# One full-precision product in place of three split ones at the head of a projection kernel

## The chip, the cores and the metric

The kernel runs on one core of a Trainium2 chip. The metric is the device time of one execution, in microseconds (us). A core has a matrix engine (TensorE; PE in the profile, with its weight loads as PEld), a vector engine (VectorE, DVE), an activation engine (ScalarE, ACT), a general engine (GpSimd, POOL) and a queue that issues transfers (SyncE, SP). Each engine works through its own list of instructions in order and waits on semaphores where an operand comes from another engine or from a transfer.

## The reference

The input x has 2048 rows of 448 numbers. Two branches are mixed by a gate per row. One is linear attention with 16 heads of 28; the other is a long convolution (a state-space layer). Cut to what matters here:

```python
q, k, v = split_heads(x @ wqkv)
pq, pk = phi(q), phi(k)              # phi(t) = where(t > 0, t + 1, exp(t)) + 1e-6
kv = einsum("bhsd,bhse->bhde", pk, v)
z  = einsum("bhsd->bhd", pk)
o  = einsum("bhqd,bhde->bhqe", pq, kv) / (einsum("bhqd,bhd->bhq", pq, z)[..., None] + 1e-6)
a  = merge_heads(o) @ wo
b  = causal_conv(x, K) + x * D_skip
g  = sigmoid((x * gate_w).sum(-1, keepdims=True))
out = g * a + (1 - g) * b
```

The part that the change touches is the k part of `x @ wqkv`, for the first 128 rows of x.

## The kernel before, in words

The 2048 rows are worked in 16 chunks of 128 (`NC`). A projection of one chunk multiplies x, turned so that its 448 columns lie on partitions, with a weight matrix of 448 rows. The 448 are cut into four tiles (`J`): tiles 1, 2 and 3 hold 128 rows each, tile 0 the last 64, held twice.

Every operand exists in two halves. The high half is the number cast to fp32r, a shorter form of which TensorE takes a product of 448 columns in 0.20 us here, where one in fp32 stands at 0.95 us in the chain; the low half is what the cast lost (`low`: number minus high half). One product in fp32 precision is then a sum of three in fp32r: high x times high w (`hh`), low x times high w (`lh`), high x times low w (`hl`). Tile 0 has both halves of w in one tile, so it needs no `hl` of its own. This makes 4 + 4 + 3 = 11 products for a projection, each with 448 columns, summed in one PSUM tile (`pieces`; `project` runs all 11).

The names that matter at the head of the program:

- `turned[c]` is the landed fp32 copy of chunk c, turned; `wkr[j]` the landed fp32 tile j of the k weights. They come in three transfers (`PARTS`): chunk 0 with tile 1, then tiles 2 and 3, then tile 0 with chunk 1.
- `xt[c]` holds the two halves of a turned chunk, `wkh` and `wkl` those of the k weights (in the trace, tiles xt and wk; landed data lie in tile y).
- `split_w(j)` casts weight tile j on ACT and calls `low_w(j)`, which takes the low half on the engine named, here DVE. `split_t(c)` casts a turned chunk on ACT and takes its low half on POOL; `split_n(c)` does the same for the chunk as it is (tile xn).
- `fill(n)` issues n dummy products of 512 columns of a bf16 tile of ones (`warm`) into an unused PSUM tile. `WARM` of them stand first on TensorE.
- `k_feature`, `k_high` and `k_low` make phi(k) of a chunk and its two halves (tiles pkh, pkl); `do_g` multiplies x with them.

The order on each engine is that of the code: the schedule is written out by hand. At the head it is: dummies; on ACT the cast of tile 1; on DVE the halves of chunk 0 and the low half of tile 1; then tiles 2, 3 and 0; the projection of chunk 0; those of chunks 1 and 2; then the features of chunk 0, and so on. The projection of chunk 0 runs in the order that `last == "w"` gives: tile 1, tile 2, the low half of tile 1, tile 3, the low halves of tiles 2 and 3, and tile 0 last. Dummies stand behind its first, second and ninth product.

Of the kernel before, what the change touches and what calls it, by code (L numbers as in the profile page):

```python
# [15 lines left out]
P = 128  # L16
S = 2048
D = 448
# [7 lines left out]
LO = NAT + D  # L26
XC = LO + 64
NX = XC - NAT + D
WARM = 9
PARTS = ((("x", 0), ("w", 1)), (("w", 2), ("w", 3)), (("w", 0), ("x", 1)))  # L30
FIRST = 2 * NAT + J * D
QA = 1
# [98 lines left out]
def gated_mix_kernel(ctx: ExitStack, tc: tile.TileContext, xin, wq_d, wv_d, wo_d, abc_d, ldt_d, dsk_d,  # L131
                     tri_d, ident_d, mask_d, gcat_d, sel_d, first_d, gin_d, lag_d, out):
    nc = tc.nc
    PE, ACT, DVE, POOL, SP = nc.tensor, nc.scalar, nc.vector, nc.gpsimd, nc.sync
# [15 lines left out]
    wkh, wkl = wk2[:, 0], wk2[:, 1]  # L150
# [31 lines left out]
    xt, xn, turned, plain = {}, {}, {}, {}  # L182
# [10 lines left out]
    wkr = {}  # L193
# [29 lines left out]
    def low(eng, o, r, h):  # L223
        eng.tensor_tensor(out=o, in0=r, in1=h.bitcast(F32), op=ALU.subtract)  # L224

    def split_t(c):
        w = xt[c] = xt_p.tile([P, 2 * NAT], F32R, name="xt", tag="t")
        ACT.copy(w[:, :NAT], turned[c])  # L228
        low(POOL, w[:, NAT:], turned[c], w[:, :NAT])

    def split_n(c):
        r, w = plain[c], xn_p.tile([P, NX], F32R, name="xn", tag="n")
        xn[c] = w
        ACT.copy(w[:, :XC - NAT], r)  # L234
        low(POOL, w[:, XC - NAT:], r[:, :D], w[:, :D])
        if c > 2:
            skip(c)

    def skip(c):
        POOL.tensor_tensor(out=y[:, c], in0=plain[c][:, :D], in1=dsk, op=ALU.mult)  # L240
# [3 lines left out]
    def fill(n):  # L244
        for _ in range(n):
            PE.matmul(idle, lhsT=warm[:, :P], rhs=warm, start=True, stop=True)  # L246

    fill(WARM)
    ACT.activation(oks, warm[:DJ, :1], AF.Exp)

    def split_w(j, h, l, w, eng):
        ACT.copy(h[:, j], w[j] if isinstance(w, dict) else w[:, j])
        low_w(j, h, l, w, eng)

    def low_w(j, h, l, w, eng):
        r = slice(0 if j else 64, P)
        w = w[j] if isinstance(w, dict) else w[:, j]
        low(eng, (l if j else h)[r, j], w[r], h[r, j])
# [44 lines left out]
    def pieces(c, wh, wl, n, tag, last=None):  # L303
        o = ps.tile([P, 512], F32, name=tag, tag=tag)
        h, l = ([xt[c][:, i + k * P:i + (k + 1) * P] for k in range(J)] for i in (0, NAT))
        hh, lh, hl = ([(a[k], w[:, k]) for k in range(J)] for a, w in ((h, wh), (l, wh), (h, wl)))
        hl = hl[1:]
        if last == "x":
            seq = hh + hl + lh
        else:  # L310
            seq = [p for k in range(J) for p in (hh[k], lh[k])] + hl
            if last == "w":
                seq = seq[2:6] + seq[8:9] + seq[6:8] + seq[9:] + seq[:2]

        def run(count):
            for _ in range(min(count, len(seq))):
                a, b = seq.pop(0)
                run.n += 1
                PE.matmul(o[:, :n], lhsT=a, rhs=b, start=run.n == 1, stop=not seq)  # L319
        run.n = 0  # L320
        return o, run

    def project(*args, **kw):
        o, run = pieces(*args, **kw)
        run(11)
        return o
# [15 lines left out]
    def k_feature(c, o):  # L342
        e = tp.tile([P, D], F32, name="e", tag="e")
        pks[c] = o[:, :D]
        ACT.activation(e, pks[c], AF.Relu, scale=-1.0)  # L345
        ACT.activation(e, e, AF.Exp, scale=-1.0)  # L346
        DVE.scalar_tensor_tensor(out=pks[c], in0=pks[c], scalar=1.0, in1=e, op0=ALU.add, op1=ALU.max)  # L347

    def k_high(c):
        pkh[c] = tp.tile([P, D], F32R, name="pkh", tag="pkh")  # L350
        ACT.add(pkh[c], pks[c], 1e-6)

    def k_low(c):
        pk = pks.pop(c)
        pkl[c] = tp.tile([P, D], F32R, name="pkl", tag="pkl")
        for o, a, op in ((pkl[c], pkh[c].bitcast(F32), ALU.subtract), (zb, zb, ALU.add))[::-1 if c == NC - 1 else 1]:
            DVE.scalar_tensor_tensor(out=o, in0=pk, scalar=1e-6, in1=a, op0=ALU.add, op1=op)
# [56 lines left out]
    w = xt[0] = xt_p.tile([P, 2 * NAT], F32R, name="xt", tag="t")  # L414
# [1 line left out]
    ACT.copy(wkh[:, 1], wkr[1])  # L416
    DVE.tensor_copy(w[:, :P], turned[0][:, :P])
    low(DVE, w[:, NAT:], turned[0], w[:, :NAT])
    low_w(1, wkh, wkl, wkr, DVE)
    for j in (2, 3, 0):  # L420
        split_w(j, wkh, wkl, wkr, DVE)
    ko, run = pieces(0, wkh, wkl, D, "k", "w")
    for n, f in ((1, 1), (1, 1), (6, 0), (1, 1), (2, 0)):
        run(n)
        fill(f)
    ko = [ko]
    split_t(1)
    ko.append(project(1, wkh, wkl, D, "v0", "x"))
    split_t(2)
    ko.append(project(2, wkh, wkl, D, "v1", "x"))  # L430
    k_feature(0, ko[0])
    k_high(0)
    split_n(0)
    k_low(0)
    k_feature(1, ko[1])
    split_n(1)
# [21 lines left out]
    for c in range(2, NC - 2):  # L458
# [9 lines left out]
        ko = project(c + 1, wkh, wkl, D, "v1" if c in (2, 4) else "k")  # L468
# [33 lines left out]
        for j in {11: (0, 1), 12: (2, 3)}.get(c, ()):  # L502
            w = xn_p.tile([P, NX], F32R, name="wo", tag="n")[:DJ, :2 * D].rearrange("p (i d) -> p i d", i=2)
# [57 lines left out]
    def gates_b(g, tag):  # L561
        n = g.shape[1]
        o = ps.tile([P, 512], F32, name="o2", tag="v1")
        PE.transpose(o[:n, :P], g, ident)
        w = tp.tile([P, D], F32R, name="phs", tag=tag)[:n, :3 * P].rearrange("p (i t) -> p i t", i=3)
        phs.append(w)
        ACT.copy(w[:, 0:2], o[:n, None, :P].to_broadcast([n, 2, P]))
        return lambda: DVE.tensor_tensor(out=w[:, 2], in0=o[:n, :P], in1=w[:, 0].bitcast(F32), op=ALU.subtract)
# [46 lines left out]
    c = NC - 2  # L615
    gate(0, c)
    ko = project(c + 1, wkh, wkl, D, "k")
# [18 lines left out]
    last = gates_b(g2, "pkl")  # L636
# [7 lines left out]
    for i in range(4):  # L644
        do_g(c + 1, (i,))
        ACT.copy(gs[i], g[i][:, :D])
    qo, q_run = pieces(c + 1, wqh, wql, D + 2, "q")
    for i in range(5):
        phi(i)
# [234 lines left out]
```

## Time and profile before

| what | value |
|---|---|
| time, median of 3 runs | 179.49 us (179.27 to 180.06) |
| the profiled execution's own time | 179.93 us |
| its span in the trace | 178.1 us |
| TensorE busy | 172.5 us, 97% of the span |
| POOL / DVE / ACT busy | 67% / 65% / 53% of the span |
| first dummy product starts | 1.47 us |
| first real product's weight load | 5.39 us |
| projection of chunk 1 begins | 8.99 us |

The time of an execution is that of the device. The span goes from the first to the last instruction that the trace shows; 179.93 - 178.1 = 1.8 us lie around it. All times of rows are counted from the span's start.

### The profile page before, as it was taken

To read this page: it belongs to the slowest core of one execution; us is meant where nothing else is said; L and a number is where in the kernel's file an instruction comes from. 1 tells how busy PE (TensorE), PEld (TensorE's weight loads), DVE (VectorE), ACT (ScalarE), POOL (GpSimd) and SP (SyncE) were. 2 spreads that over 40 slices of the span, in tenths; PEclk is the share of its full clock that TensorE was granted. 3 is DMA by queue.
4 is the path that set the end of the run, shared out by engine and by line. 5 is a ranking of instruction groups with operands and counts; after the bars stand their busy time and mean duration, and the time that the engine had idled before them with its cause. 6 is when DMAs were issued, how large, how long until landed. Compare 5 with 4: busy or idle time off the path is not lost.

```text
span 178.1 us, 2750 instructions
## 1 busy us (share of the span) xinstructions
PE 172.5 (97%) x879; PEld 152.0 (85%) x879; DVE 115.9 (65%) x238; ACT 94.7 (53%) x212; POOL 119.5 (67%) x124
## 2 busy tenths in 40 slices
PE   6999999999999999999999999999999999999991
PEld 2598999999999999999989999877879999899990
DVE  1747647688857173562824519389799999998551
ACT  3779388884537244372536653444565455564441
POOL 3167577879259969687598999059289998773100
PEclk9999999999999999999999999999999999999999
DMA  5999974198003303033033000000031221131222
GB/s 166 416 291 271 249 203 153 10 375 239 4 1 118 118 0 120 5 118 101 18 118 122 0 0 0 0 4 5 6 60 68 88 98 62 67 119 73 109 76 82
DMA packets 7784, 18.40 MB, mean 103 GB/s; under 512 B 1755, under 2 KB 4520, under 8 KB 7768
## 3 DMA queue, kind: packets, MB, share of 16 engines
q1 hardware_dynamic: 7720, 18.16, 32.2%
q8 instruction: 7, 0.11, 0.3%
q10 hardware_dynamic: 48, 0.06, 0.2%
q14 instruction: 9, 0.07, 0.1%
HBM read 14.20 MB, written 3.67 MB: 100 GB/s over the span
## 4 chain that ended last, share of the span: by engine, by line
PE 91%; DVE 5%; issue 1%; ACT 1%; ACTq 0%
PE g L388 20%; PE q L319 19%; PE a L602 16%; PE k L319 15%; PE v L319 6%; PE tr L577 3%; PE q L246 3%; PE v L396 2%; PE v L395 2%; PE m L671 1%; DVE th L585 1%; DVE ot L607 1%; DVE den L527 1%; DVE den L522 1%; PE tr L691 1%
## 5 line engine op out<-in xcount | busy, mean ns | idle before, releaser
L602 PE MATMUL a<-wk,th 128*128 128x448 f32 (+1 forms) x170 | 39.5, 364 | 0.0
L388 PE MATMUL g<-pkh,xn 128*128 128x448 f32 x112 | 36.1, 370 | 0.0
L602 PEld LDWEIGHTS a<-wk,th 128*128 128x128 f32 x170 | 29.6, 189 | 2.6 <-DMA wk<-shl 0.3
L319 PE MATMUL k<-wk,xt 128*128 128x448 f32 x132 | 30.4, 376 | 0.0
L347 DVE SCALAR_TENSOR_TENSOR k<-k,e 128x448 f32<-128x448 f32 x12 | 7.6, 632 | 33.9 <-ACT e L346 33.9
L319 PE MATMUL q<-wqh,xt 128*128 128x450 f32 x120 | 27.7, 368 | 0.0
L319 PEld LDWEIGHTS k<-wk,xt 128*128 128x128 f32 x132 | 25.1, 190 | 2.9 <-ACT wk L416 0.8
L407 POOL TENSOR_TENSOR y<-y,t 128x448 f32<-128x448 f32 x16 | 18.6, 1163 | 13.4 <-DVE t L400 13.1
L224 POOL TENSOR_TENSOR xn<-xr,xn 128x448 fp32r<-128x448 f32 x16 | 19.2, 1200 | 8.7 <-ACT xn L234 8.4
L319 PEld LDWEIGHTS q<-wqh,xt 128*128 128x128 f32 x120 | 22.7, 189 | 2.7 <-issue 0.7
L517 POOL TENSOR_TENSOR prod<-pq,zb 128x448 f32<-128x448 f32 x16 | 18.6, 1162 | 8.3 <-ACT zb L629 6.0
L388 PE MATMUL g<-pkl,xn 128*128 128x448 f32 x64 | 23.5, 367 | 0.0
L388 PEld LDWEIGHTS g<-pkh,xn 128*128 128x128 f32 x112 | 21.1, 188 | 2.8 <-issue 0.2
L345 ACT ACTIVATE e<-k 128x448 f32<-128x448 f32 x12 | 6.5, 545 | 30.2 <-PE k L319 30.2
L240 POOL TENSOR_TENSOR y<-xr,rows 128x448 f32<-128x448 f32 x16 | 18.7, 1168 | 0.0
L224 POOL TENSOR_TENSOR xt<-xr,xt 128x512 fp32r<-128x512 f32 x14 | 18.3, 1306 | 0.2 <-ACT xt L228 0.2
L540 POOL TENSOR_TENSOR pn<-pq,den 128x336 f32<-128x336 f32 x16 | 12.1, 754 | 7.7 <-DVE den L529 5.6
L584 ACT CAST th<-tr 128x512 fp32r<-128x512 f32 x16 | 9.4, 589 | 9.2 <-PE tr L577 9.0
L607 DVE SCALAR_TENSOR_TENSOR ot<-y,og,a 128x448 f32<-128x448 f32 (+1 forms) x17 | 10.4, 615 | 4.6 <-PE a L602 4.6
L613 ACT COPY pq<-a 128x448 f32<-128x448 f32 (+1 forms) x17 | 8.8, 517 | 6.5 <-DVE ot L607 5.7
L388 PEld LDWEIGHTS g<-pkl,xn 128*128 128x128 f32 x64 | 11.2, 175 | 1.2 <-issue 0.2
L319 PE MATMUL q<-wql,xt 128*128 128x450 f32 x45 | 11.7, 364 | 0.0
(135 smaller groups left out, 305.0 us busy)
## 6 DMA issues: line engine op xcount, KB each, us to landing
xr<-in SPq DMA_DIRECT2D x15, 512.0 KB, 3.5
out<-ot SPq DMA_DIRECT2D x15, 224.0 KB, 1.9
pq<-in SPq DMA_DIRECT2D x4, 448.0 KB, 13.3
y<-in SPq DMA_DIRECT2D x2, 480.0 KB
y<-in SPq DMA_DIRECT2D x2, 450.0 KB, 7.4
wv<-in SPq DMA_DIRECT2D x1, 896.0 KB, 5.5
wo<-in SPq DMA_DIRECT2D x1, 784.0 KB
y<-in SPq DMA_DIRECT2D x1, 448.0 KB
```

The source lines that it names most:

```text
L224: eng.tensor_tensor(out=o, in0=r, in1=h.bitcast(F32), op=ALU.subtract)
L240: POOL.tensor_tensor(out=y[:, c], in0=plain[c][:, :D], in1=dsk, op=ALU.mult)
L319: PE.matmul(o[:, :n], lhsT=a, rhs=b, start=run.n == 1, stop=not seq)
L347: DVE.scalar_tensor_tensor(out=pks[c], in0=pks[c], scalar=1.0, in1=e, op0=ALU.add, op1=ALU.max)
L388: PE.matmul(g[i][:a.shape[1], :D], lhsT=a, rhs=b, start=c == 0 and n == 0, stop=c == NC - 1 and n == len(seq) - 1)
L407: POOL.tensor_tensor(out=y[:, c], in0=y[:, c], in1=t, op=ALU.add)
L517: POOL.tensor_tensor(out=pd[c], in0=pq[:, c], in1=zb, op=ALU.mult)
L540: POOL.tensor_tensor(out=n[:, :3, :DJ].rearrange("p j (h d) -> p j h d", h=4), in0=a, in1=r[:, :H - 4].rearrange("p (j h) -> p j h", j=3)[ ...
L584: ACT.copy(h, ov)
L602: PE.matmul(a[:, lo:hi], lhsT=u_, rhs=w_[:, lo:hi], start=n == 0, stop=n == 10)
L607: DVE.scalar_tensor_tensor(out=ot[:, lo:hi], in0=y[:, c, lo:hi], scalar=og[:, c:c + 1], in1=a[:, lo:hi], op0=ALU.mult, op1=ALU.add)
L613: ACT.copy(pq[:, c, lo:hi], a[:, lo:hi])
```

## The change

For chunk 0, the three split products of tile 1 (high with high, low with high, high with low) become one product of the landed fp32 operands, which needs no split and waits for the first transfer alone. The other eight products follow in the order tile 2, tile 3, the low halves of tiles 2 and 3, tile 0. The dummy products among them go, and one of the nine ahead of them. The low half of weight tile 1, which chunks 1 and later still use, is taken behind the low halves of the other tiles. On ACT the cast of `split_n(0)` moves ahead of `k_high(0)`.

```diff
-WARM = 9
+WARM = 8
...
             if last == "w":
                 seq = seq[2:6] + seq[8:9] + seq[6:8] + seq[9:] + seq[:2]
+            elif last == "r":
+                seq = [(turned[c][:, P:2 * P], wkr[1])] + seq[4:8] + seq[9:] + seq[:2]
...
-    low_w(1, wkh, wkl, wkr, DVE)
     for j in (2, 3, 0):
         split_w(j, wkh, wkl, wkr, DVE)
-    ko, run = pieces(0, wkh, wkl, D, "k", "w")
-    for n, f in ((1, 1), (1, 1), (6, 0), (1, 1), (2, 0)):
-        run(n)
-        fill(f)
-    ko = [ko]
+    ko = [project(0, wkh, wkl, D, "k", "r")]
+    low_w(1, wkh, wkl, wkr, DVE)
...
     k_feature(0, ko[0])
+    split_n(0)
     k_high(0)
-    split_n(0)
     k_low(0)
```

The rows below are instructions in program order. The part in brackets is what an instruction waits for: DMAHW0 is a transfer's semaphore, DVE, Activation and Pool those of the engines. The tile k is the PSUM tile of chunk 0, v_176 (v_170 after) that of chunk 1, and q that of the dummies.

TensorE, from the last dummy of the opening to the first products of chunk 1, before:

```order
L246 MATMUL q<-warm 128x512
L319 MATMUL k<-wk_69,xt 128x448 [waits DVE_49,Activation_49]
L246 LDWEIGHTS warm
L246 MATMUL q<-warm 128x512
L319 MATMUL k<-wk_69,xt 128x448 [waits DVE_49]
...
L319 MATMUL k<-wk_69,xt 128x448 [waits DVE_49] x2
L246 LDWEIGHTS warm
L246 MATMUL q<-warm 128x512
L319 MATMUL k<-wk_69,xt 128x448 [waits DVE_49]
L319 MATMUL k<-wk_69,xt 128x448
L319 MATMUL v_176<-wk_69,xt 128x448 [waits Activation_49]
```

The same place after:

```order
L246 MATMUL q<-warm 128x512
L321 MATMUL k<-y 128x448 [waits DMAHW0_49]
L321 MATMUL k<-wk_69,xt 128x448 [waits DVE_49,Activation_49]
L321 MATMUL k<-wk_69,xt 128x448 [waits DVE_49]
L321 MATMUL k<-wk_69,xt 128x448 [waits Activation_49]
L321 MATMUL k<-wk_69,xt 128x448
L321 MATMUL k<-wk_69,xt 128x448 [waits DVE_49] x3
L321 MATMUL k<-wk_69,xt 128x448
L321 MATMUL v_170<-wk_69,xt 128x448 [waits Activation_49]
L321 MATMUL v_170<-wk_69,xt 128x448 x3
L321 MATMUL v_170<-wk_69,xt 128x448 [waits DVE_49]
```

The first product of k reads the landed tile y and waits for the transfer only; eight products of the split operands stand behind it with no dummy between, and the fifth product of chunk 1 (high x with the low half of tile 1) now waits for DVE.

DVE, at the same time, before:

```order
L224 TENSOR_TENSOR xt<-y,xt 128x512 [waits DVE_49]
L224 TENSOR_TENSOR wk_69<-y,wk_69 128x448 [waits Activation_49]
L224 TENSOR_TENSOR wk_69<-y,wk_69 128x448 [waits DMAHW1_49,Activation_49]
L224 TENSOR_TENSOR wk_69<-y,wk_69 128x448 [waits Activation_49]
L224 TENSOR_TENSOR wk_69<-y,wk_69 64x448 [waits DMAHW2_49,Activation_49]
L347 SCALAR_TENSOR_TENSOR k<-k,e 128x448 [waits Activation_49]
```

and after:

```order
L224 TENSOR_TENSOR xt<-y,xt 128x512 [waits DVE_49]
L224 TENSOR_TENSOR wk_69<-y,wk_69 128x448 [waits DMAHW1_49,Activation_49]
L224 TENSOR_TENSOR wk_69<-y,wk_69 128x448 [waits Activation_49]
L224 TENSOR_TENSOR wk_69<-y,wk_69 64x448 [waits DMAHW2_49,Activation_49]
L224 TENSOR_TENSOR wk_69<-y,wk_69 128x448
L349 SCALAR_TENSOR_TENSOR k<-k,e 128x448 [waits Activation_49]
```

The low half of tile 1 has gone from ahead of tiles 2 and 3 to behind the 64 rows of tile 0; the number of operations is the same.

ACT, from the cast of chunk 2 on, before:

```order
L228 CAST xt<-xr 128x512
L345 ACTIVATE e<-k 128x448
L346 ACTIVATE e<-e 128x448
L351 ACTIVATE pkh<-k 128x448
L234 CAST xn<-xr 128x512
L345 ACTIVATE e<-v_176 128x448
```

and after:

```order
L228 CAST xt<-xr 128x512
L347 ACTIVATE e<-k 128x448
L348 ACTIVATE e<-e 128x448
L234 CAST xn<-xr 128x512
L353 ACTIVATE pkh<-k 128x448
L347 ACTIVATE e<-v_170 128x448
```

The cast of chunk 0's untransposed copy (xn) and the high half of its features (pkh) have changed places.

## The prediction

> **What bounds the kernel now.** I read the page first, then TensorE's waits, then the chain that ended last, then the first 14 us of the timeline in narrow windows. The page's span, busy shares and chain by engine:
>
> ```profile
> span 178.1 us, 2750 instructions
> PE 172.5 (97%) x879; PEld 152.0 (85%) x879; DVE 115.9 (65%) x238; ACT 94.7 (53%) x212; POOL 119.5 (67%) x124
> PE 91%; DVE 5%; issue 1%; ACT 1%; ACTq 0%
> ```
>
> TensorE is busy nearly all the time and carries the chain. The view of its waits has two rows (total, times, longest):
>
> ```profile
> PE q L246 <- DVE warm L178: 1.5, 1, 1.5
> PE tr L577 <- DVE pn L543: 0.2, 1, 0.2
> ```
>
> So what TensorE does at the head is passed on to the end, unless a later chain takes over. The chain in order of time (start, length, what) shows the head and the one place where it leaves TensorE:
>
> ```profile
> 1.47 4.02 PE q L246 x9
> 5.49 0.65 PE k L319
> 6.14 0.45 PE q L246
> 6.59 0.37 PE k L319
> 6.96 0.33 PE q L246
> 7.29 1.43 PE k L319 x7
> 8.71 0.23 PE q L246
> 8.95 0.41 PE k L319 x2
> 9.35 4.49 PE v L319 x22
> ...
> 141.63 0.45 PE tr L577 x4
> ...
> 142.16 0.60 ACT th L584
> ```
>
> From 142 us ACT and DVE hold the chain for some 10 us, but what starts them there is a transpose on TensorE (141.63 us). A TensorE that runs earlier by some tenths starts them earlier by as much. So I expect a shift at the head to reach the end whole, and the question is how much earlier the projection of chunk 1 begins.
>
> The head in the timeline (start, length, engine and line, operands; in brackets the idle time before it and what ended it):
>
> ```profile
> 2.30 0.15 PEld L246 LDWEIGHTS <-warm 128*128 128x128 bf16 x1 [0.28 <-issue]
> 2.73 0.15 PEld L246 LDWEIGHTS <-warm 128*128 128x128 bf16 x1 [0.28 <-issue]
> 4.43 1.06 PE L246 MATMUL q<-warm 128*128 128x512 bf16 x2
> 4.78 0.57 ACT L416 CAST wk<-y 128x448 fp32r<-128x448 f32 x1 [2.53 <-DMA y<-in]
> 5.39 0.29 PEld L319 LDWEIGHTS k<-wk,xt 128*128 128x128 f32 x1 [0.81 <-ACT wk L416]
> 6.33 0.56 ACT L252 CAST wk<-y 128x448 fp32r<-128x448 f32 x1
> 6.76 0.15 PEld L246 LDWEIGHTS <-warm 128*128 128x128 bf16 x1 [0.42 <-issue]
> 7.06 0.57 ACT L252 CAST wk<-y 128x448 fp32r<-128x448 f32 x1 [0.17 <-DMA y<-in]
> 7.12 0.19 PEld L319 LDWEIGHTS k<-wk,xt 128*128 128x128 f32 x1
> 7.66 0.62 DVE L224 TENSOR_TENSOR wk<-y,wk 64x448 fp32r<-64x448 f32 x1
> 8.55 0.10 PEld L246 LDWEIGHTS <-warm 128*128 128x128 bf16 x1 [0.22 <-issue]
> 8.99 0.19 PEld L319 LDWEIGHTS v<-wk,xt 128*128 128x128 f32 x1
> ```
>
> Three things are to be seen. First, TensorE changes its pace: a weight load of a dummy takes 0.15 us until 6.76 and 0.10 us at 8.55, one of a real product 0.29 us at 5.39 and 0.19 us at 7.12. So up to about 7.1 us it is slow. (The clock line of the page does not show this; it stands at full throughout.) At the slow pace dummies of 512 columns follow each other every 2.73 - 2.30 = 0.43 us, which for 448 columns is 0.43 x 448/512 = 0.37 us; at the full pace the 22 products of chunks 1 and 2 take 4.49 us, 0.204 us each. Second, data arrive in steps: the first transfer before 4.78, the last part of the weights at 7.06. Its cast on ACT ends at 7.63, its low half on DVE at 7.66 + 0.62 = 8.28; before that, the last two products (tile 0) can't start. Third, from 7.12 to 8.99 nothing waits: products and a dummy run back to back, and tile 0's data are there before TensorE comes to them. So before the change the head is bound by TensorE itself: the slow pace, the two split products and two dummies ahead of 7.1, and a third dummy behind.
>
> **The change part by part.** *The dummy ahead and the first product.* The last two of the nine dummies are the row at 4.43; the last one starts 0.43 later, at 4.86, so eight end at 4.86 on TensorE. The first transfer has landed by 4.78. The fp32 product waits for nothing else, so its weight load starts at about 4.87, 0.5 us ahead of 5.39. Its price is not in the head of the trace; the nearest rows are other fp32 products, both at the full pace, in the chain:
>
> ```profile
> 116.08 0.95 PE zo L627 x2
> 122.30 1.57 PE k L691 x16
> ```
>
> L627 is one fp32 product of the same shape, 128 x 448, shown as two records: 0.95 us. L691 is eight products of 112 columns, two records each: 1.57/8 = 0.196 us, so 0.785 us for 448 columns. The slow pace takes 0.43 us for 512 columns and the full one 0.204 x 512/448 = 0.233, so it is 1.85 times as long: 1.45 to 1.75 us. The weight load of 0.29 us lies before it. The bounds for the end are thus 4.87 + 0.785 = 5.7 (if the pace were full) and 4.87 + 0.29 + 1.75 = 6.9 us. I take 6.9, since the pace was slow until 7.1 in the trace. Before the change TensorE had the second split product behind it at that point and one dummy in front: it came to tile 2 at 7.12.
>
> *Tile 2, tile 3 and their low halves.* Tile 2's cast is done by 6.33 (the cast of tile 3 starts there), tile 3's at 6.33 + 0.56 = 6.89. DVE's work doesn't get earlier by the removed step: its low halves wait for ACT's casts, and that of tile 0 starts at 7.66, right behind the cast that ends at 7.63. Six products stand here, before the wait for tile 0: one half at the slow pace until 7.1, then 5.5 x 0.204 = 1.1 us, so they end at 8.2. With the fp32 product at 5.7 they would be done earlier, and the next step is the same.
>
> *Tile 0.* DVE ends at 8.28. From ACT's end at 4.78 + 0.57 = 5.35 to the load at 5.39 there are 0.04 us, so the first load of tile 0 is at 8.32. This is the new wait: TensorE stands from 8.2, with 0.1 us of idle time and a bare weight load of 0.19. Behind it are only TensorE's own products, and all of them wait. The second load follows 0.2 us later, and the first of chunk 1 0.2 us after that, at 8.72. Before it was at 8.99. **The gain is 0.27 us.** Bounds: if the weight load isn't bare, the same; if the fp32 product took twice the 0.95 us, 1.9, the six products would end at 8.3, and the gain would still be 0.2. Above, the data set 8.32 whatever TensorE does, so in this execution not more than 0.3.
>
> *What is given up as cover.* Of the 0.27 us, the hl product and the third dummy, 0.2 us each, are the work that goes from behind 7.1; the wait for DVE eats the rest. The dummies had hidden nothing that the trace shows.
>
> *The moved steps.* The low half of tile 1 now follows on DVE at 8.28 and ends at about 8.9. Its user is the fifth product of chunk 1, at 8.72 + 4 x 0.2 = 9.5: hidden, with 0.6 to spare. Behind it on DVE is the feature of chunk 0, whose end ACT waits for at 11.24, two us later: no one waits. The rows that bear on chunk 1's low x and on the swap on ACT are:
>
> ```profile
> 8.29 1.29 POOL L224 TENSOR_TENSOR xt<-y,xt 128x512 fp32r<-128x512 f32 x1 [5.96 <-ACT xt L228]
> 8.35 0.62 ACT L228 CAST xt<-xr 128x512 fp32r<-128x512 f32 x1 [0.20 <-DMA xr<-in]
> 11.24 0.55 ACT L351 ACTIVATE pkh<-k 128x448 fp32r<-128x448 f32 x1 [0.70 <-DVE k L347]
> 11.69 0.61 ACT L234 CAST xn<-xr 128x512 fp32r<-128x512 f32 x1
> 11.82 0.62 DVE L357 SCALAR_TENSOR_TENSOR pkl<-k,pkh 128x448 fp32r<-128x448 f32 x1 [0.61 <-ACT pkh L351]
> 13.49 0.19 PEld L388 LDWEIGHTS g<-pkh,xn 128*128 128x128 f32 x1
> ```
>
> POOL has chunk 1's low x at 9.58; its first user is the eighth product, at 8.72 + 7 x 0.2 = 10.1. The cast of xn takes 0.61 us and goes into 0.70 us in which ACT waited for DVE: nothing is late, and POOL gets xn sooner, since the cast starts at 11.24 - 0.70 - 0.27 = 10.27 and not at 11.69. pkh and pkl are wanted at 13.49 - 0.27 = 13.2 and were there at 12.44 already. The cast's data share a transfer with chunk 2, landed by 8.35; were the cover gone, pkh would be 0.6 us later and still in time. No transfer is moved or added: SP's list is the same.
>
> *Sum.* 179.93 - 0.27 = 179.66 us against the profiled execution's own time, which is 0.44 above the median; against the median 179.49 - 0.27 = 179.2 us, 0.15% less. A measurement of this kernel can tell about 0.5%, 0.9 us, from no change.
>
> **The rivals.** *The slow pace lasts longer (slower).* Between the dummy at 1.47 and the first full-speed load at 7.12 TensorE had 5.65 us of nearly unbroken work. If the fp32 product does not count for that, or the dummies' absence breaks it, the count begins anew at its end: slow until 6.9 + 5.65 = 12.5 us. Each product costs 0.37 instead of 0.204; 5.6 us hold 15 slow ones, which cost 15 x 0.17 = 2.5 us more than full ones, of which the wait for tile 0 would have hidden 0.4. Against before that is 2.1 - 0.27, about +1.8 us: 181.3. It decides from where the pace rises 1.25 us later than it did, at 8.35 us: by then four slow products are done, 4 x 0.37 from 6.9, and the other four end at 8.35 + 4 x 0.204 = 9.2, where before chunk 1 began at 9.19 by the same count (8.99 and the load). For it: the dummies that go had kept TensorE at work in this very stretch. Against it: TensorE is empty only for some tenths after the change (8.2 to 8.32), less than the gap that ends at 5.39 before it, which the pace survived. I give it 0.15.
>
> [...]
>
> *The pace rises at another moment in the executions that are timed.* The three times before differ by 0.8 us, more than the gain. If it rises earlier, by 6 us, TensorE reaches tile 0 early in both kernels, both stand until 8.32, and the gain is nothing: 179.5. I give it 0.17. If it rises later, at 8.3, the old head, with 1.6 us of slow work more in it, is late by 1.2 x (1 - 0.204/0.37) = 0.55 us, while the new one has four full products left, 8.3 + 0.85 = 9.17 against 9.74: the gain is 0.57, 178.9. I give it 0.13. [...]
>
> **How the numbers follow.** The forecast, 179.2, has 0.52; no gain 0.17; the larger gain 0.13; the slower head 0.15; 0.03 is left for what I don't see. Below 178.6 (faster by over 0.5%) lies the far part of the larger gain, with the spread of the times: 0.08. Above 180.4 lies most of the slower head: 0.14. The rest, 0.78, is within 0.5%. The range goes from 178.6, the larger gain with 0.3 of spread, to 180.6: midway between the moment from which the slower head decides (no change) and its far end (181.3) lies 180.4, to which 0.2 of spread is added; only the far half of that rival is left out, some 0.07, and as much below.
>
> **What would show it.** In the profile after: one load of k from tile y at about 4.87, its two records ending near 6.9; six products with no dummy; an idle time before a load of k at about 8.32 that is ended by DVE's row of 64 partitions; the first load of v at 8.7; then all later rows 0.27 earlier, with DVE's chain near 142 us shifted alike. It is wrong if loads of k or v still take 0.29 us behind 7.5 us, if chunk 1 begins at 8.99 or later, or if TensorE's waits get a row in chunk 1 (DVE's low half of tile 1, or POOL).

## The result, and the profile after

| kernel | median | range | runs |
|---|---|---|---|
| before | 179.50 us | 179.22 to 180.06 | 20 |
| changed | 179.97 us | 179.74 to 180.51 | 20 |

The ratio is 1.0028, with a 95% interval of 1.0020 to 1.0037: the changed kernel is 0.5 us slower, where the forecast was 0.27 us faster. The difference is small, less than 0.5%, but clear of the noise.

The page's head and three rows of TensorE's waits, of the changed kernel. TensorE now has waits at the head, one of them in chunk 1 (`v`) for DVE:

```profile
span 178.2 us, 2740 instructions
PE 171.5 (96%) x874; PEld 151.0 (85%) x874; DVE 117.2 (66%) x238; ACT 94.8 (53%) x212; POOL 119.8 (67%) x124
...
PE k L321 <- ACT wk L252: 0.4, 1, 0.4
PE v L321 <- DVE wk L224: 0.3, 1, 0.3
...
PE k L321 <- DVE wk L224: 0.2, 1, 0.2
```

The chain that ended last runs at the head through DVE, with one piece of 1.75 us:

```profile
7.02 0.58 ACT wk L252
...
7.62 0.62 DVE wk L224
...
8.28 1.75 DVE wk L224
...
10.07 3.93 PE v L321 x18
```

The timeline of the changed kernel shows what that piece is:

```profile
4.75 0.50 PEld L321 LDWEIGHTS k<-y 128*128 128x128 f32 x2 [0.59 <-DMA y<-in]
6.44 0.19 PEld L321 LDWEIGHTS k<-wk,xt 128*128 128x128 f32 x1 [1.19 <-ACT wk L252]
8.25 1.29 POOL L224 TENSOR_TENSOR xt<-y,xt 128x512 fp32r<-128x512 f32 x1 [5.91 <-ACT xt L228]
8.28 1.74 DVE L224 TENSOR_TENSOR wk<-y,wk 128x448 fp32r<-128x448 f32 x1
8.30 0.30 PEld L321 LDWEIGHTS k<-wk,xt 128*128 128x128 f32 x2 [0.48 <-DVE wk L224]
8.61 0.80 PEld L321 LDWEIGHTS v<-wk,xt 128*128 128x128 f32 x4
9.50 1.68 POOL L224 TENSOR_TENSOR xt<-xr,xt 128x512 fp32r<-128x512 f32 x1
10.07 3.55 PEld L321 LDWEIGHTS v<-wk,xt 128*128 128x128 f32 x18 [0.66 <-DVE wk L224]
13.64 0.19 PEld L390 LDWEIGHTS g<-pkh,xn 128*128 128x128 f32 x1
```

Tile 0 is multiplied from 8.30 and chunk 1 begins at 8.61, earlier than the 8.99 of before. Then the moved operation, the low half of tile 1, takes 1.74 us on DVE instead of 0.62. It starts at 8.28, just behind POOL's low half of chunk 1 (8.25), which runs until 9.54, and it ends half a microsecond after that. POOL's next operation takes 1.68 us where it took 1.29 before. The fifth product of chunk 1, for which 9.5 was forecast, starts at 10.07, and `do_g(0)` at 13.64 instead of 13.49.

### The profile page after: what moved, and what is told of

It reads as the page before. It is cut to its first block, busy times and chain, and to the rows that moved or that the text cites. A ratio compares the mean times of both kernels' runs of the same rounds, so it can differ in the third digit from the quotient of the medians.

```text
span 178.2 us, 2740 instructions
## 1 busy us (share of the span) xinstructions
PE 171.5 (96%) x874; PEld 151.0 (85%) x874; DVE 117.2 (66%) x238; ACT 94.8 (53%) x212; POOL 119.8 (67%) x124
## 4 chain that ended last, share of the span: by engine, by line
PE 73%; DVE 10%; issue 5%; ACT 4%; DMA 3%; POOL 2%; SPq 0%; ACTq 0%; POOLq 0%
PE q L321 16%; PE g L390 16%; PE a L600 15%; PE k L321 13%; PE v L321 6%; DMA y<-in 3%; PE tr L575 3%; DVE den L520 2%; PE v L398 2%; PE v L397 2%; DVE den L525 2%; DVE pn L541 1%; DVE wk L224 1%; DVE th L583 1%; DVE ot L605 1%
## 5 line engine op out<-in xcount | busy, mean ns | idle before, releaser
L321 PE MATMUL k<-wk,xt 128*128 128x448 f32 x129 | 28.8, 369 | 0.6 <-ACT wk L252 0.4
L321 PEld LDWEIGHTS k<-wk,xt 128*128 128x128 f32 x129 | 24.0, 188 | 4.1 <-ACT wk L252 1.4
```

## The experiments

Theory A: DVE's low half of tile 1, at its new place, meets POOL's low half of chunk 1; the two can't work side by side, DVE is held until POOL is through, and chunk 1 waits for it. Theory B: that long operation is hidden or long for another reason, and the loss is in the fp32 product, in the missing dummies or in a later chain.

**Low half of tile 1 put back** (`e1_low_first`).

```diff
+    low_w(1, wkh, wkl, wkr, DVE)
     for j in (2, 3, 0):
         split_w(j, wkh, wkl, wkr, DVE)
     ko = [project(0, wkh, wkl, D, "k", "r")]
-    low_w(1, wkh, wkl, wkr, DVE)
```

> The changed kernel with one step put back: DVE takes the low half of tile 1 ahead of tiles 2 and 3 again. Theory A (the low half of tile 1 met POOL's low half of chunk 1 on the way to SBUF and took 1.75 us instead of 0.62): no wait in chunk 1, its fifth product starts near 9.45 instead of 10.07 us, do_g(0) near 13.0 instead of 13.64, time 179.35 us, 0.6 below the changed kernel and about 0.1 below the one before. Theory B (the loss is in the fp32 product or in a later chain, and the row of 1.75 us is hidden): within 0.1 us of the changed kernel, 179.9 to 180.0.

Measured: 179.44 us, ratio to the kernel before 0.9989 (0.9977 to 1.0002). The timeline has four low halves on DVE in one stretch, and the 22 products of chunks 1 and 2 in another, without a wait:

```profile
5.64 2.39 DVE L224 TENSOR_TENSOR wk<-y,wk 128x448 fp32r<-128x448 f32 x4
8.09 0.30 PEld L321 LDWEIGHTS k<-wk,xt 128*128 128x128 f32 x2 [0.48 <-DVE wk L224]
8.40 4.48 PEld L321 LDWEIGHTS v<-wk,xt 128*128 128x128 f32 x22
```

The place of this one operation is worth 179.97 - 179.44 = 0.53 us, all of the loss. This is what theory A expects.

**POOL held back** (`e2_pool_behind`).

```diff
     low_w(1, wkh, wkl, wkr, DVE)
+    POOL.tensor_tensor(out=late, in0=turned[1][:, :16], in1=wkl[:, 1, :16].bitcast(F32), op=ALU.subtract)
     split_t(1)
```

Here `late` is a new tile of 16 numbers per partition.

> The changed kernel with POOL held back: a small POOL operation that reads the low half of tile 1 stands ahead of POOL's low half of chunk 1, so that the two large operations can't overlap. DVE's own order is that of the changed kernel. Theory A: DVE's operation takes 0.62 us again and ends at 8.9; POOL's starts at about 9.1 and ends at 10.4; chunk 1 waits for POOL at its eighth product, at 10.4 instead of 10.04, so 0.25 to 0.4 us less is lost than in the changed kernel: 179.6 to 179.75 us. Theory B, and any theory by which the operation is long for its own sake or for the transfers under way: it still takes about 1.7 us, POOL ends near 11.4, and the time is 180.9.

Measured: 180.08 us, ratio 1.0027 (1.0016 to 1.0038). The view by line gives all four of DVE's low halves (shortest, median, longest in ns), and the timeline the new wait:

```profile
L225 DVE TENSOR_TENSOR wk<-y,wk x4: 617/623/628, 6.2 to 8.1; 128x448 fp32r<-128x448 f32 x3, 64x448 fp32r<-64x448 f32 x1
...
9.04 1.30 POOL L225 TENSOR_TENSOR xt<-y,xt 128x512 fp32r<-128x512 f32 x1
10.39 2.90 PEld L322 LDWEIGHTS v<-wk,xt 128*128 128x128 f32 x15 [0.55 <-POOL xt L225]
13.30 0.19 PEld L391 LDWEIGHTS g<-pkh,xn 128*128 128x128 f32 x1
```

At the same place, and with POOL out of the way, the operation takes 0.62 us: the duration is as theory A has it. The time is not: the head is 0.34 us earlier than in the changed kernel (13.30 against 13.64), but the lead is gone by 103 us: from 29 us on, the loads of each projection take 2.26 us in this trace and 2.22 or 2.23 in that of the changed kernel.

**The same without a new tile** (`e5_pool_behind_same_map`): `late` is replaced by a part of the existing tile `sm`, of 112 partitions.

> As e2_pool_behind, but the small POOL operation writes into a tile that exists already, so that no tile after it lies elsewhere in SBUF. In e2 do_g(0) began at 13.30, 0.34 earlier than in the changed kernel, as theory A has it, but the lead was gone by 105 us, a little in every projection from 27 us on. If the added tile's shift of the addresses did that (theory C), projections take 2.24 us here as in the changed kernel, the lead stays, and the time is 179.6 to 179.7 us. If it comes from POOL's later start (theory D), this run loses its lead in the same way: 180.0 to 180.1 us.

Measured: 179.97 us, ratio 1.0025 (1.0013 to 1.0037).

```profile
L224 DVE TENSOR_TENSOR wk<-y,wk x4: 618/624/626, 6.3 to 8.2; 128x448 fp32r<-128x448 f32 x3, 64x448 fp32r<-64x448 f32 x1
...
10.51 2.94 PEld L321 LDWEIGHTS v<-wk,xt 128*128 128x128 f32 x15 [0.54 <-POOL xt L224]
13.46 0.19 PEld L390 LDWEIGHTS g<-pkh,xn 128*128 128x128 f32 x1
```

The operation is short again, and this time the lead stays: 0.18 us at 13.46, 0.17 in the projection of k at 102.91 (103.08 in the changed kernel). So in these two traces the added tile goes with the lost lead; why, these runs don't show, and the medians, 180.08 and 179.97 us, hardly tell the two kernels apart. The expected time was too low all the same. Holding POOL back moves the wait from the fifth product to the eighth, and the end of chunk 1 moves little: 10.07 + 7 x 0.204 = 11.50 in the changed kernel, 10.51 + 4 x 0.204 = 11.33 here, of which 0.06 is data that landed earlier. A tenth is left, which the times don't resolve.

**One operand from PSUM** (`e9_psum_operand`).

```diff
-    low_w(1, wkh, wkl, wkr, DVE)
+    DVE.scalar_tensor_tensor(out=wkl[:, 1], in0=idle[:, :D], scalar=1e-6, in1=wkr[1], op0=ALU.add, op1=ALU.subtract)
```

> The changed kernel with DVE's late operation at its place, of the same size and with the same output tile, but with one operand from PSUM (the dummies' tile) in place of the cast of tile 1, so that one operand comes from SBUF and not two. The low half of tile 1 is thereby not computed; the rest is. Theory A (two SBUF operands on DVE meet POOL's): it takes 0.62 us beside POOL's operation, the fifth product of chunk 1 doesn't wait, do_g(0) begins near 13.0, time 179.45 us as e1. If any late DVE operation is held up there (by place, by the transfers under way): 1.7 us again and 179.95 us.

Measured: 179.41 us, ratio 0.9993 (0.9978 to 1.0008).

```profile
7.89 0.56 ACT L252 CAST wk<-y 128x448 fp32r<-128x448 f32 x1 [1.13 <-DMA y<-in]
9.11 1.30 POOL L224 TENSOR_TENSOR xt<-y,xt 128x512 fp32r<-128x512 f32 x1 [6.77 <-ACT xt L228]
9.14 0.62 DVE L424 SCALAR_TENSOR_TENSOR wk<-q,y 128x448 fp32r<-128x448 f32 x1
9.47 4.48 PEld L321 LDWEIGHTS v<-wk,xt 128*128 128x128 f32 x22
```

This is the cleanest of the runs: the same place, the same size, POOL's operation beside it all the time, and 0.62 us with one operand less from SBUF. Nothing in chunk 1 waits. (In the execution that was profiled, the third transfer landed late, at 7.89, and the rows behind it are 0.9 us later; its own time was 180.49, the longest of twelve.) The rival that any late operation is held up there has fallen.

The instruction is of another kind too, SCALAR_TENSOR_TENSOR in place of TENSOR_TENSOR. The changed kernel's own trace shows that the kind is not what matters. There a TENSOR_TENSOR of DVE, with one operand from PSUM (v), takes 0.61 us wholly inside an operation of POOL:

```profile
54.63 1.15 POOL L409 TENSOR_TENSOR y<-y,t 128x448 f32<-128x448 f32 x1
55.10 0.61 DVE L402 TENSOR_TENSOR t<-v,rows 128x448 f32<-128x448 f32 x1
```

**Low half of tile 1 on POOL** (`e3_low_pool`): at the place of e1, with POOL in place of DVE.

> The changed kernel with the low half of tile 1 on POOL, which is idle at 5.3 us, instead of on DVE. Theory A: the two engines meet earlier: POOL's operation runs from 5.95 (behind DVE's low half of chunk 0) to 7.1, DVE's low half of tile 2 can't start before that and takes some 1.2 us by its row, all of DVE's low halves are 0.55 later, tile 0 is multiplied from 8.85 and chunk 1 begins at 9.15: about 179.9 us, no better than the changed kernel. Theory B: the engines don't disturb each other, chunk 1 begins at 8.61 and nothing waits: 179.35 us.

Measured: 179.70 us, ratio 1.0010 (0.9997 to 1.0023): between the two theories' numbers. The engines do meet:

```profile
5.31 1.53 POOL L224 TENSOR_TENSOR wk<-y,wk 128x448 fp32r<-128x448 f32 x1 [2.98 <-ACT wk L418]
6.29 1.03 DVE L224 TENSOR_TENSOR wk<-y,wk 128x448 fp32r<-128x448 f32 x1 [0.46 <-ACT wk L252]
```

POOL's operation, which starts while DVE's low half of chunk 0 runs (5.14 to 5.83), takes 1.53 us, where one of 448 columns at 11.31 takes 1.15 in the same trace; DVE's low half of tile 2 takes 1.03, where the low half of tile 0 takes 0.62. But the delay of 0.4 us is smaller than expected, and part of it is hidden. In the profiled execution, the longest of the twelve with 180.04 us, the third transfer landed only at 7.58, and tile 0 waited for that. DVE was through with tile 3 at 6.29 + 1.56 = 7.85 us (1.56 is the row of its low halves of tiles 2 and 3 together). In the changed kernel tile 0's low half started at 7.62, so where the transfer is not late some 0.2 us are lost by this estimate; the medians of this run and e1 are 0.26 apart.

**The other parts of the change.** `e6_split_no_dummies` is e1 with the order of the kernel before, `"w"` for `"r"`: no fp32 product, no dummies.

> e1_low_first with the fp32 product taken out again: chunk 0's projection in the order of the kernel before, 11 split products, but with no dummies between them and eight ahead. It tells what the fp32 product itself brings. Theory A says that the head now waits for the low half of tile 0 at about 8.3 whatever stands ahead: chunk 1 begins at 8.6 as in e1, time within 0.1 us of e1, 179.45. If the fp32 product is what brings the gain, or if an idle TensorE between 4.9 and 5.4 us delays the rise of its pace, chunk 1 begins 0.3 us later or more: 179.75 and up.

`e7_swap_only` is the kernel before with `split_n(0)` ahead of `k_high(0)`.

> The kernel before with nothing changed but the swap on ACT: the cast of split_n(0) ahead of k_high(0). The prediction priced it at nothing: 179.5 us, within 0.1 of the kernel before; POOL gets xn of chunk 0 more than 1 us sooner.

`e8_dummies_back` is e1 with two dummies.

```diff
-    ko = [project(0, wkh, wkl, D, "k", "r")]
+    ko, run = pieces(0, wkh, wkl, D, "k", "r")
+    for n, f in ((1, 1), (6, 1), (2, 0)):
+        run(n)
+        fill(f)
+    ko = [ko]
```

> e1_low_first with two dummy products put back: one behind the fp32 product, one ahead of tile 0. If they stand where TensorE waits anyway (0.4 us behind the fp32 product, 0.2 ahead of tile 0 in e1's trace), they cost nothing while the pace rises early: 179.45 us, and at most 0.2 us in an execution in which it rises late.

Measured: 179.47 us for e6 (ratio 1.0002, 0.9983 to 1.0021), 179.40 for e7 (1.0003, 0.9992 to 1.0014), 179.39 for e8 (1.0000, 0.9991 to 1.0009). The three medians came out as expected. (One of e6's twelve executions took 181.11 us; no trace shows why.) In e6's timeline the head ends at the same wait for DVE as e1's, without the fp32 product:

```profile
8.18 0.30 PEld L321 LDWEIGHTS k<-wk,xt 128*128 128x128 f32 x2 [0.71 <-DVE wk L224]
8.49 4.48 PEld L321 LDWEIGHTS v<-wk,xt 128*128 128x128 f32 x22
```

So the fp32 product, the dummies and the swap are each worth nothing that the medians tell.

**The kernel before, once more** (`e4_before_again`).

> The kernel before once more, for a second trace of its head. If its profiled execution was one in which the pace of TensorE rose late (7.1 us), another one may show it earlier: then tile 0 waits for DVE at about 8.3 and chunk 1 begins near 8.7 instead of 8.99. If the pace always rises at the same moment, chunk 1 begins at 8.99 again. Time 179.5 us either way.

Measured: 179.50 us; the profiled execution took 179.41 us, with a span of 177.6.

```profile
5.90 0.29 PEld L319 LDWEIGHTS k<-wk,xt 128*128 128x128 f32 x1
6.48 0.10 PEld L246 LDWEIGHTS <-warm 128*128 128x128 bf16 x1 [0.29 <-issue]
8.57 4.48 PEld L319 LDWEIGHTS v<-wk,xt 128*128 128x128 f32 x22
13.07 0.19 PEld L388 LDWEIGHTS g<-pkh,xn 128*128 128x128 f32 x1
```

The pace rises between 5.90 and 6.48 us here, not at 7.1, and chunk 1 begins at 8.57, as early as in the changed kernel. The changed kernel's `do_g(0)`, at 13.64, is 0.57 us later than this. In e7, which has the same head, a load takes 0.19 us at 5.23 already. The execution behind the prediction's profile, 179.93 us with chunk 1 at 8.99, was one of the long ones. Such executions are common: 44 of the 129 timed executions of the kernel before, e4's twelve included, took 179.7 us or more. Whether the pace rose late in the others too is not shown, since only this one of them was profiled.

**A version that might beat both** (`e10_two_full`), and e1 beside it (`e11_low_first_again`).

```diff
-                seq = [(turned[c][:, P:2 * P], wkr[1])] + seq[4:8] + seq[9:] + seq[:2]
+                seq = [(turned[c][:, P:2 * P], wkr[1])] + seq[4:8] + [(turned[c][:64, :P], wkr[0][:64])] + seq[9:]
...
-            seq = hh + hl + lh
+            seq = hh[1:] + hh[:1] + hl + lh
```

> A version that could beat both: e1_low_first with tile 0 too multiplied as one fp32 product, from the landed data of rows 0 to 63, ahead of the low halves of tiles 2 and 3, and with tile 0 last among the high products of chunk 1. Chunk 0 then no longer waits for DVE at about 8.1 to 8.3: four products end at 7.3, the fp32 product of tile 0 at 8.1, the two low halves at 8.5 by TensorE's own pace; chunk 1's first load is at 8.3 to 8.4 instead of 8.4 to 8.6. Theory A gives 0.1 to 0.2 us less than e1: 179.3 us, hardly to be told from it. If the fp32 product of half the rows is dearer than 0.8 us, no gain.

> e1_low_first once more, beside the two others on the same chip: 179.45 us, chunk 1 at 8.4 to 8.6, no wait in chunk 1.

Measured: 179.61 us for e10 (1.0000, 0.9988 to 1.0012) and 179.42 for e11 (0.9992, 0.9982 to 1.0002). Of e10:

```profile
7.53 0.29 PEld L321 LDWEIGHTS k<-y 64*128 64x128 f32 x2 [0.31 <-DMA y<-in]
8.48 0.30 PEld L321 LDWEIGHTS k<-wk,xt 128*128 128x128 f32 x2 [0.65 <-issue]
8.79 4.48 PEld L321 LDWEIGHTS v<-wk,xt 128*128 128x128 f32 x22
```

The fp32 product of half the rows takes 8.48 - 7.53 = 0.95 us from load to load, as dear as L627's chain row for the full height, and it had to wait for the third transfer. No gain. e1 and e11, both with 179.4, lie 0.1 us below the kernel before, with intervals that just reach no change; no version here has a clearly better median.

The long executions are another matter. Of the 47 executions of e1, e8, e9 and e11, which all have the fp32 product and no wait in chunk 1, 5 took 179.7 us or more, against the 44 of 129. A head that depends less on when the pace rises would give that. But the mark of 179.7 was chosen after the times were known, e10, with the fp32 product, has 3 of 12, and e6 and e7, without it, 4 of 12 each: a gain in the long executions is possible and not shown.

## Why the prediction was wrong

*The step that failed is the one on the moved steps.* It priced the low half of tile 1 at 0.62 us, from 8.28 to 8.9, and called it hidden with 0.6 us to spare. It took 1.74 us, to 10.02, and chunk 1 waited for it. The measured 179.97 us are 0.77 above the forecast of 179.2: by e1's 179.44, 0.53 of that belong to this step, and 0.24 to a gain that the median doesn't have (below). The row that it collided with, POOL's at 8.29, stood in the same paragraph, quoted for another purpose: each operation was priced as if the other weren't there. The profile of before has a row that shows the price. On DVE, 450 columns from two SBUF operands take 0.62 us with POOL free for most of it, and 1.26 us when POOL's operation of 17.12 is already running:

```profile
16.68 0.62 DVE L224 TENSOR_TENSOR wql<-y,wqh 128x450 fp32r<-128x450 f32 x1
17.12 1.21 POOL L224 TENSOR_TENSOR wql<-y,wqh 128x450 fp32r<-128x450 f32 x1 [0.81 <-ACT wqh L252]
17.55 1.26 DVE L224 TENSOR_TENSOR wqh<-y,wqh 64x450 fp32r<-64x450 f32 x1 [0.24 <-ACT wqh L252]
```

The runs show what the collision takes: 1.74 us beside POOL in the changed kernel, 0.62 with POOL held back (e2, e5), 0.62 beside POOL with one input from PSUM (e9). When DVE's operation started, POOL's had 1.26 us left in the changed kernel (8.28 to 9.54), 0.78 in the kernel before (17.55 to 18.33) and 0.55 in e3 (6.29 to 6.84). DVE's ended 0.48 us after POOL's end each time, at 10.02, 18.81 and 7.32. That fits a wait for the end and not a sharing. What the two engines meet at, and why the second operand from SBUF matters, no run here shows.

*The gain of 0.27 us* was read in one of the long executions of the kernel before and does not hold for the median. Against its 8.99 the changed kernel's 8.61 is even a little better than the forecast 8.72. But in the other two traces of the old head, e4 and e7, chunk 1 begins at about 8.6 too. The rival "no gain, the pace rises earlier", which had 0.17, describes the median: e1, which has the forecast's head without the collision, is 0.1 us faster and not 0.27.

*What held.* Tile 0's products wait for DVE: forecast 8.32, measured 8.30. That the time fits so well is luck, since it moves with the landing of the third transfer, from 8.07 in e8's trace to 9.16 in e9's. The swap on ACT costs nothing that the median tells (e7: 179.40 us, ratio 1.0003). The head's shift reaches the end: in twelve of the thirteen profiled executions, the time is 166.3 to 166.5 us more than the start of `do_g(0)`, from 12.86 us in e8 (179.19) to 13.97 in e9 (180.49); only e2 has 166.7. So the 0.57 us by which the changed kernel's `do_g(0)` is later than e4's are 0.54 us of time in these two executions (179.95 and 179.41). The slower head of the forecast, a pace that stays slow behind the fp32 product, did not come: the load at 6.44 takes 0.19 us. That unbroken work is what brings the rise, as that rival supposed, no run shows. The changed kernel is slower by another mechanism. The prediction named a wait for DVE's low half of tile 1 as a sign of being wrong, but gave it no price and no chance among its rivals. (One sum of the rivals is off: 8.3 + 0.85 is 9.15 and not 9.17, which changes neither the forecast nor the range.)

*The fp32 product* had no part in the error. Its load started at 4.75. Its two loads took 0.50 us, about a slow one of 0.29 and a fast one of 0.19, so the pace seems to have risen while they ran. TensorE then waited for tile 2's cast until 6.44. Whether the product ends at 6.0, as the trace has it, or at the forecast 6.9 does not matter, because tile 0 is the later wait.

## What to carry to other kernels

An operation that is moved on one engine has to be held against what the engines beside it do at the new place: look for rows of the same form in the profile that took twice as long, and see what ran beside them. For DVE with two SBUF operands that neighbour is POOL in these runs (1.03, 1.26 and 1.74 us in place of 0.62). And where the head of a kernel depends on a moment that shifts between executions, here the rise of TensorE's pace (by 5.23 us in e7's trace, by 7.12 in that of the kernel before) and the landing of a transfer (by 6.80 in e8's, by 7.89 in e9's), take a gain from more than one execution, and from those near the median first.

## What the runs showed of the hardware

TensorE's pace, by its weight loads, rose between 6.76 and 7.12 us in one execution of the kernel before, between 5.90 and 6.48 in another, and between 4.44 and 5.23 in e7's; the mean granted clock of these executions was 0.999, 0.998 and 0.995. The third transfer of the head landed by 6.80 us in e8's trace, by 7.02 in the changed kernel's and by 7.89 in e9's. Three low halves of DVE, with two SBUF operands, that started while an operation of POOL ran ended 0.48 us after POOL's end, whether 0.55 (e3), 0.78 (the kernel before) or 1.26 us (the changed kernel) of that were left. POOL's operations were longer beside DVE's too: its low half of chunk 2, started at 9.50 with DVE's long operation running until 10.02, took 1.68 us, and 1.29 in the kernel before.
